# Windowed attention, forward and backward: the gradient's tile loads issued from the GpSimd queue in place of the SyncE queue

## The chip, the cores and the metric

The kernel runs on one core of one Trainium2 chip. A core has a matrix engine (PE, with its weight loads PEld), a vector engine (DVE), a scalar engine (ACT), GpSimd (POOL) and SyncE (SP), each with an instruction queue of its own that it works through in program order. DMAs are started by an instruction in one of these queues. The metric is the device time of one execution in microseconds (us); lower is better. Times are medians of several executions; the profile is of one execution.

## The reference

The input `x` is an image of 256 x 256 positions with C = 384 channels in bf16. It is cut into 8 x 8 windows of 64 positions, and each window does single-head attention; the kernel returns the output and, for a given `grad_out` of the same shape as `x`, the gradients with respect to `x`, `wqkv` and `wo`.

```python
xw  = windows(x)                       # (1024 windows, 64, 384)
qkv = xw @ wqkv                        # wqkv: (384, 1152)
q, k, v = split(qkv, 3)
p   = softmax(q @ k.T * C ** -0.5)     # 64 x 64 in each window
o   = unwindow((p @ v) @ wo)           # wo: (384, 384)
return o, *vjp(x, wqkv, wo)(grad_out)
```

## The kernel before

**Weights.** The products of weights that the windows need are formed once at the start: A = Wq Wk^T (scaled), B = Wv Wo, and their transposes AT and BT. With them the scores of a window are x A x^T, the output is P (x B), and the backward pass needs grad_out BT and x AT.

**Tiles and quads.** A tile is two windows one above the other: 16 image rows by 8 columns, 128 positions on the 128 partitions, 384 channels along the free dimension. Four tiles side by side make a quad. There are 16 bands of 32 tiles, so 512 tiles and 128 quads; `quads` (L328) lists them and `sts` holds the state of each.

**One quad's work.** `load` (L112 to L118) fetches a quad's four tiles of `x` into `xq` (L117) and its four tiles of `grad_out` into `dq` (L118), 96 KB a DMA. `load_turn` (L120 to L128) issues two DMA transposes (L127), `dT` from `dq` and `xT` from `xq`, both with the channels on the partitions. `project` (L140) multiplies `dT` by BT (kind 0) and `xT` by A (kind 1) into `yz`; ACT copies the results from PSUM (L150 for kind 0, L152 for kind 1). `to_tokens` (L154) issues a third, double-sized DMA transpose, `tok` from `yz` (L156). `scores` (L159, matmuls on L165) takes `yz` and `xT`; `soft` is the softmax and its backward on DVE and ACT; `uv` (L212, matmuls on L219) makes x B and x AT; `turn` transposes small squares on PE; `attend` (L235) makes the output and the gradient of `x` for two of the four tiles. It copies each from PSUM with ACT into the buffers `osb` (L259) and `dsb` (L263), of which the pool `ob` keeps three each, and stores each in two halves of 48 KB from POOL (L266). `gf_group` (L271) adds up the weights' gradients for groups of three quads and is fed in between by `filler`.

**The order.** The whole main loop stands under a manual schedule (L332): every engine works in exactly the order in which the code is written. Iteration i of the loop (L339 to L350) issues `load` for quad i+3, `load_turn` for quad i+2, and then one `step` in which three quads are at different stages: the quad i+1 is projected (A), the quad i goes through scores, softmax and the first half of `attend` (B), the quad i-1 through the second half of `attend` (C). The projection from `dT` comes in the middle of a step, after the `uv` matmuls (L313), and `to_tokens` near its end (L322). In the queue of SP an iteration is therefore eight tile loads, the transposes dT and xT, and the transpose tok. In the queue of POOL a step is the eight half-tile stores of the second half of `attend` for quad i-1, followed by the eight of the first half for quad i.

**Buffers.** `xq` has 10, `dq` 6, `xT` 3, `dT`, `yz` and `tok` 2 buffers. PSUM is a ring of eight banks (`ring`) that all matmul results pass through.

**Semaphores.** A DMA's landing is told by one of eight semaphores for the DMAs of SP (DMAHW0 to 7) and one of eight for those of POOL (DMASW0 to 7), taken in turn. A DMA waits, beside its data, for the landing of the DMA of its own queue that had the same semaphore, eight DMAs earlier.

Of the kernel before, what the change touches and what calls it, by code (L numbers as in the profile page):

```python
# [22 lines left out]
def kernel(  # L23
# [21 lines left out]
    nc = tc.nc  # L45
# [60 lines left out]
    def dram_tile(ap, bp, t):  # L106
        return ap[0, 2 * WIN * bp:2 * WIN * (bp + 1), WIN * t:WIN * (t + 1), :]
# [4 lines left out]
    def load(st):  # L112
        bp, t0 = st["at"]
        st["xq"] = xq = grp.tile([P, QUAD, C], BF16, tag="xq", name="xq", bufs=2 * GQ + 4)
        st["dq"] = dq = qp.tile([P, QUAD, C], BF16, tag="dq", name="dq", bufs=6)
        for t in range(QUAD):
            nc.sync.dma_start(out=xq[:, t, :], in_=dram_tile(x, bp, t0 + t))  # L117
            nc.sync.dma_start(out=dq[:, t, :], in_=dram_tile(grad_out, bp, t0 + t))  # L118

    def load_turn(st):  # L120
        xq, dq = st["xq"], st["dq"]
# [210 lines left out]
    with tc.manual_schedule(engines=MANUAL):  # L332
        for i in range(min(AHEAD, n)):
            load(sts[i])
            if i < AHEAD - 1:
                load_turn(sts[i])
        held = []
        get = lambda i: sts[i] if 0 <= i < n else None
        for i in range(-1, n + 1):  # L339
            if AHEAD <= i + AHEAD < n:  # L340
                load(sts[i + AHEAD])
            if AHEAD - 1 <= i + AHEAD - 1 < n:
                load_turn(sts[i + AHEAD - 1])
            step(get(i - 1), get(i), get(i + 1))
            if i > 0:
                held.append(sts[i - 1])
                sts[i - 1] = None
            if held and (len(held) == GQ or i == n):
                fill.append(gf_group(held))
                held = []  # L350
        filler(1 << 30)
# [60 lines left out]
```

## Time and profile before

| what | before |
|---|---|
| device time, median of 3 | 2145.26 us (2143.43 to 2146.45) |
| span of the profiled execution | 2144.9 us |
| busy PE / DVE / ACT / POOL | 95% / 64% / 68% / 53% |
| mean granted PE clock | 0.995 |
| DMA, mean over the span | 191 GB/s, 409.04 MB in 1046330 packets |

The profiled execution's span lies 0.4 us below the median of the timed runs and within their range; nothing else lies around it, so terms taken from the span can be set against the median. SP is not in the first table of the page, because everything that it does is issuing and counts as no busy time; its instructions are seen in the timeline and in the views of single lines. In those views the three numbers after a count are the shortest, the median and the longest duration in ns. In the timeline a row is: start in us, duration in us, engine, line, operation, names, count, and in brackets the idle time of the engine ahead of it with what ended it.

### The profile page before, as it was taken

Reading aid. Unit: us, or ns where it says so; the run is one execution under the profiler, and the core shown is the slowest. Engines: PE = TensorE matmul, PEld = TensorE weight load, DVE = VectorE, ACT = ScalarE, POOL = GpSimd, SP = SyncE. Lnnn points to the kernel's source line nnn. Section 1 sums busy time; section 2 is a strip of 40 time slices with the busy share of each in tenths; the row PEclk is TensorE's granted clock in tenths of the full one; section 3 lists DMA queues with packets and bytes.
Section 4 is the critical chain, followed back from the end, with each engine's and each line's share of the span. In section 5 each row is a group of like instructions: output and inputs, shape, how many; then the busy total and the mean of one; then the engine's idle time right before and its main releaser. Section 6 shows DMA issues by size and latency. Waiting matters only on the chain.

```text
span 2144.9 us, 50954 instructions
## 1 busy us (share of the span) xinstructions
PE 2029.8 (95%) x18814; PEld 1098.6 (51%) x18814; DVE 1379.5 (64%) x3235; ACT 1448.5 (68%) x3213; POOL 1137.8 (53%) x2054
## 2 busy tenths in 40 slices
PE   7899999999999999999999999999999999999998
PEld 4455555555555555555545555554555555455544
DVE  4566666666666666666666666666666666666665
ACT  5676676767666766666766767676766667676663
POOL 1555555555555555555554555555555455555544
PEclk9999999999999999999999999999999999999999
DMA  8999999999999999999999999999999999999992
GB/s 171 198 192 197 192 196 196 192 193 199 193 193 196 200 191 195 191 196 193 198 190 190 198 191 202 193 197 188 197 198 196 190 198 194 192 198 194 190 184 76
DMA packets 1046330, 409.04 MB, mean 191 GB/s; under 512 B 880704, under 2 KB 1028928, under 8 KB 1046080
## 3 DMA queue, kind: packets, MB, share of 16 engines
q1 hardware_dynamic: 947376, 304.17, 80.9%
q0 software_dynamic: 98304, 101.32, 18.2%
q8 instruction: 147, 2.41, 0.5%
q14 instruction: 103, 0.84, 0.1%
q10 hardware_dynamic: 400, 0.29, 0.0%
HBM read 101.84 MB, written 101.84 MB: 95 GB/s over the span
## 4 chain that ended last, share of the span: by engine, by line
PE 41%; DMA 26%; SPq 15%; ACT 9%; issue 5%; POOL 1%; DVE 1%; ACTq 0%; POOLq 0%
DMA dT<-dq 20%; PE pj L147 16%; PE pj L219 10%; PE pg L278 9%; SPq L117 7%; SPq L118 7%; DMA out_dram<-osb 5%; ACT yz L150 4%; ACT osb L259 3%; PE sd L165 3%; POOL out_dram L266 1%; SPq L156 1%; DMA out_dram<-dsb 1%; ACT yz L152 1%; PE pd L244 1%
## 5 line engine op out<-in xcount | busy, mean ns | idle before, releaser
L266 POOL DMA_DIRECT2D out_dram<-osb x1024 | 571.9, 563 | 933.6 <-ACT osb L259 906.3
L266 POOL DMA_DIRECT2D out_dram<-dsb x1024 | 571.9, 563 | 51.2 <-issue 20.5
L259 ACT CAST osb<-po 128x384 bf16<-128x384 f32 x512 | 249.8, 488 | 408.4 <-DMA out_dram<-osb 180.6
L280 DVE TENSOR_TENSOR GF_acc<-pg,GF_acc 128x384 f32<-128x384 f32 x258 | 143.9, 558 | 542.7 <-PE pg L278 542.7
L278 PEld LDWEIGHTS <-xq 128*128 128x128 bf16 x3072 | 300.0, 98 | 226.8 <-issue 1.6
L219 PEld LDWEIGHTS <-xT 128*128 128x128 bf16 x3072 | 291.9, 98 | 185.5 <-issue 3.6
L219 PE MATMUL pj<-B_sb,xT 128*128 128x384 bf16 x1536 | 334.6, 327 | 1.8 <-ACT dsb L263 1.8
L219 PE MATMUL pj<-AT_sb,xT 128*128 128x384 bf16 x1536 | 334.0, 327 | 0.0
L147 PE MATMUL pj<-dT,BT_sb 128*128 128x512 bf16 x1152 | 276.6, 387 | 60.4 <-DMA dT<-dq 54.2
L260 DVE CAST Uq<-pu 128x384 bf16<-128x384 f32 x512 | 283.0, 553 | 75.3 <-PE pu L251 75.3
L267 DVE CAST Wq<-pw 128x384 bf16<-128x384 f32 x512 | 280.5, 548 | 0.0
L221 ACT CAST uq<-pj 128x384 bf16<-128x384 f32 x512 | 247.5, 483 | 41.9 <-PE pj L219 37.5
L278 PE MATMUL pg<-Uq,xq 128*128 128x384 bf16 x1536 | 270.5, 326 | 0.1
L278 PE MATMUL pg<-Wq,xq 128*128 128x384 bf16 x1536 | 270.1, 326 | 0.1
L147 PE MATMUL pj<-xT,A_sb 128*128 128x512 bf16 x1152 | 269.2, 379 | 0.6
L263 ACT CAST dsb<-pd 128x384 bf16<-128x384 f32 x512 | 254.7, 497 | 7.6 <-DMA out_dram<-dsb 6.4
L221 ACT CAST vq<-pj 128x384 bf16<-128x384 f32 x512 | 250.2, 489 | 2.8 <-PE pj L219 0.5
L152 ACT CAST yz<-pj 128x512 bf16<-128x512 f32 x384 | 224.2, 585 | 32.0 <-PE pj L147 0.9
L150 ACT CAST yz<-pj 128x512 bf16<-128x512 f32 x384 | 208.4, 638 | 14.4 <-PE pj L147 13.3
L147 PEld LDWEIGHTS <-BT_sb 128*128 128x128 bf16 x1152 | 106.8, 99 | 207.2 <-DMA dT<-dq 92.2
L198 ACT COPY ps<-Pb 64x256 bf16<-64x256 bf16 x256 | 103.2, 403 | 149.6 <-DVE Pb L195 148.1
L251 PE MATMUL pu<-xq,ST 64*64 64x384 bf16 x1024 | 175.5, 336 | 0.0
(64 smaller groups left out, 2217.4 us busy)
## 6 DMA issues: line engine op xcount, KB each, us to landing
xq<-in_x_dram SPq DMA_DIRECT2D x512, 96.0 KB, 3.2
dq<-in_grad_out_dram SPq DMA_DIRECT2D x512, 96.0 KB, 3.3
out_dram<-osb POOLq DMA_DIRECT2D x1024, 48.0 KB, 3.8
out_dram<-dsb POOLq DMA_DIRECT2D x1024, 48.0 KB, 4.4
dT<-dq SPq DMA_TRANSPOSE x128, 6.5
xT<-xq SPq DMA_TRANSPOSE x128, 7.1
tok<-yz SPq DMA_TRANSPOSE x128, 7.9
w_sb<-in_wqkv_dram SPq DMA_DIRECT2D x1, 864.0 KB, 5.5
```

Source lines behind the costliest of these rows:

```text
L147: nc.tensor.matmul(pj[:].rearrange("p t w k -> p (t w k)"), lhsT=wgt[:, m, mo * P:(mo + 1) * P], rhs=src[:, :, m, :], start=(m == 0), stop ...
L150: ENG[EV["z"][mo]](out=yz[:, mo, :, 0:4:3, :], in_=pj[:])
L152: ENG[EV["y"][mo]](out=yz[:, mo, :, 1:3, :], in_=pj[:])
L219: nc.tensor.matmul(pj[:], lhsT=st["xT"][:, t, m, :], rhs=wgt[:, m, :], start=(m == 0), stop=(m == CK - 1))
L221: cp(out=dst[:, t, :], in_=pj[:])
L251: nc.tensor.matmul(dst[o, :], lhsT=st[lhs][h, t, :], rhs=st[rhs][h, t, :], start=first, stop=True)
L259: ENG[EV["o"][t]](out=osb[:], in_=po[:])
L260: ENG[EV["U"][t]](out=st["Uq"][:, t, :], in_=pu[:])
L263: ENG[EV["d"][t]](out=dsb[:], in_=pd[:])
L266: nc.gpsimd.dma_start(out=dram_tile(dst, bp, t0 + t)[WIN * w:WIN * (w + 1)], in_=src[h, :])
L267: ENG[EV["W"][t]](out=st["Wq"][:, t, :], in_=pw[:])
L278: nc.tensor.matmul(pw[:], lhsT=st["xq"][:, t, ma * P:(ma + 1) * P], rhs=st["UW"[f] + "q"][:, t, :], start=(i == 0), stop=(i == n - 1))
```

## The change

The four DMAs that fetch a quad's tiles of `grad_out` are issued from the queue of POOL (`nc.gpsimd`) in place of the queue of SP (`nc.sync`). The call stays where it is in the code, at the start of an iteration.

```diff
         for t in range(QUAD):
             nc.sync.dma_start(out=xq[:, t, :], in_=dram_tile(x, bp, t0 + t))
-            nc.sync.dma_start(out=dq[:, t, :], in_=dram_tile(grad_out, bp, t0 + t))
+            nc.gpsimd.dma_start(out=dq[:, t, :], in_=dram_tile(grad_out, bp, t0 + t))
```

In the queue of SP, one iteration in the middle of the program before, with what each instruction waits for (DMAHW and DMASW are the semaphores of SP's and POOL's DMAs):

```order
L156 DMA_TRANSPOSE tok<-yz 128x24x128 [waits DMAHW6_49,Activation_49]
L117 DMA xq<-in_x_dram 128x1x384 [waits DMAHW7_49,PE_49]
L118 DMA dq<-in_grad_out_dram 128x1x384 [waits DMAHW0_49]
L117 DMA xq<-in_x_dram 128x1x384 [waits DMAHW1_49]
L118 DMA dq<-in_grad_out_dram 128x1x384 [waits DMAHW2_49]
L117 DMA xq<-in_x_dram 128x1x384 [waits DMAHW3_49]
L118 DMA dq<-in_grad_out_dram 128x1x384 [waits DMAHW4_49]
L117 DMA xq<-in_x_dram 128x1x384 [waits DMAHW5_49]
L118 DMA dq<-in_grad_out_dram 128x1x384 [waits DMAHW6_49]
L127 DMA_TRANSPOSE dT<-dq 128x12x128 [waits DMAHW7_49]
```

The same stretch of SP's queue with the change:

```order
L156 DMA_TRANSPOSE tok<-yz 128x24x128 [waits DMAHW7_49,Activation_49]
L117 DMA xq<-in_x_dram 128x1x384 [waits DMAHW0_49]
L117 DMA xq<-in_x_dram 128x1x384 [waits DMAHW1_49]
L117 DMA xq<-in_x_dram 128x1x384 [waits DMAHW2_49]
L117 DMA xq<-in_x_dram 128x1x384 [waits DMAHW3_49]
L127 DMA_TRANSPOSE dT<-dq 128x12x128 [waits DMASW7_49,DMASW6_49,DMAHW4_49,DMASW5_49,DMASW4_49]
L127 DMA_TRANSPOSE xT<-xq 128x12x128 [waits DMAHW5_49]
```

Between tok and dT there are four loads where there were eight, and dT now waits for landings of POOL's DMAs.

In the queue of POOL, at the border between two steps, before (the last four stores of one step, the first four of the next):

```order
L266 DMA out_dram<-osb 8x8x384 [waits DMASW0_49,Activation_49]
L266 DMA out_dram<-osb 8x8x384 [waits DMASW1_49]
L266 DMA out_dram<-dsb 8x8x384 [waits DMASW2_49,Activation_49]
L266 DMA out_dram<-dsb 8x8x384 [waits DMASW3_49]
L266 DMA out_dram<-osb 8x8x384 [waits DMASW4_49,Activation_49]
L266 DMA out_dram<-osb 8x8x384 [waits DMASW5_49]
L266 DMA out_dram<-dsb 8x8x384 [waits DMASW6_49,Activation_49]
L266 DMA out_dram<-dsb 8x8x384 [waits DMASW7_49]
```

And with the change:

```order
L266 DMA out_dram<-osb 8x8x384 [waits DMASW4_49,Activation_49]
L266 DMA out_dram<-osb 8x8x384 [waits DMASW5_49]
L266 DMA out_dram<-dsb 8x8x384 [waits DMASW6_49,Activation_49]
L266 DMA out_dram<-dsb 8x8x384 [waits DMASW7_49]
L118 DMA dq<-in_grad_out_dram 128x1x384 [waits DMAHW3_49,DMASW0_49,PE_49]
L118 DMA dq<-in_grad_out_dram 128x1x384 [waits DMASW1_49]
L118 DMA dq<-in_grad_out_dram 128x1x384 [waits DMASW2_49]
L118 DMA dq<-in_grad_out_dram 128x1x384 [waits DMASW3_49]
L266 DMA out_dram<-osb 8x8x384 [waits DMASW4_49,Activation_49]
L266 DMA out_dram<-osb 8x8x384 [waits DMASW5_49]
L266 DMA out_dram<-dsb 8x8x384 [waits DMASW6_49,Activation_49]
L266 DMA out_dram<-dsb 8x8x384 [waits DMASW7_49]
```

The four loads of a later quad stand between the last store of one step and the first store of the next, in a queue that is worked through in order. At the program's start sixteen of them, for the first four quads, stand ahead of POOL's first store. Nothing changes in the order on PE, DVE and ACT.

## The prediction

> **What bounds the kernel now.** I read the page first, by engine and by chain.
>
> ```profile
> PE 2029.8 (95%) x18814; PEld 1098.6 (51%) x18814; DVE 1379.5 (64%) x3235; ACT 1448.5 (68%) x3213; POOL 1137.8 (53%) x2054
> PE 41%; DMA 26%; SPq 15%; ACT 9%; issue 5%; POOL 1%; DVE 1%; ACTq 0%; POOLq 0%
> ```
>
> PE is busy for 95% of the span, so at most 2144.9 - 2029.8 = 115 us can be won without less work on PE. But the chain that ended last stands in DMAs and in SP's queue for 41% of the span. The chain of waits in order of time shows a step where PE waits for nothing, from one quad's scores to the next, and after it one where it waits:
>
> ```profile
> 998.50 0.59 ACT yz L152
> ...
> 1018.20 6.65 DMA dT<-dq
> ...
> 1024.90 2.12 PE pj L147 x9
> ...
> 1068.20 0.86 PE sd L165 x24
> ...
> 1083.99 0.86 PE sd L165 x24
> ```
>
> The step without a wait takes 1083.99 - 1068.20 = **15.79 us**. The projection at 1024.90 starts just when the transpose dT, issued at 1018.20, lands 6.65 us later. The first and last scores say what a step takes on the average, and the same view for tok says it for SP:
>
> ```profile
> L165 PE MATMUL sd<-xT,yz x3072: 188/193/243, 20.6 to 2102.3; 128*128 128x64 bf16 x192
> L156 SPq DMA_TRANSPOSE tok<-yz x128: 3603/5592/7426, 30.2 to 2099.0; - x128
> L127 SPq DMA_TRANSPOSE dT<-dq x128: 1439/2204/3315, 9.7 to 2076.3; - x128
> L127 SPq DMA_TRANSPOSE xT<-xq x128: 1715/2778/4687, 11.4 to 2077.8; - x128
> L118 SPq DMA_DIRECT2D dq<-in_grad_out_dram x512: 552/598/1852, 2.0 to 2065.0; - x171
> ```
>
> The last scores matmul starts about 0.7 us into its step, so a step is (2101.6 - 20.6)/127 = 16.39 us, 0.60 us above 15.79. SP goes from tok to tok in (2099.0 - 30.2)/127 = 16.29 us. It is never idle in between:
>
> ```profile
> 1006.75 6.27 SPq L156 DMA_TRANSPOSE tok<-yz  x1
> 1013.06 0.59 SPq L117 DMA_DIRECT2D xq<-in_x_dram  x1
> ...
> 1018.20 2.17 SPq L127 DMA_TRANSPOSE dT<-dq  x1
> 1020.42 1.99 SPq L127 DMA_TRANSPOSE xT<-xq  x1
> 1022.51 5.35 SPq L156 DMA_TRANSPOSE tok<-yz  x1
> ```
>
> Eight loads lie between 1013.06 and dT at 1018.20, 0.64 us each; from the end of an instruction to the next 0.04 to 0.1 us pass. By the program dT is issued a whole step ahead of its use; here it is issued 6.7 us ahead, because **SP's queue has fallen behind**. PE needs 15.79 us a step, SP 16.29, and PE, gaining on SP, waits now and then.
>
> One row of the waits speaks against this reading:
>
> ```profile
> SPq L156 <- ACT yz L150: 578.1, 115, 6.3
> ```
>
> It says that tok, 5 us a step, waits for ACT. But tok waits for the last copy of its quad, on L152, and that copy ended at 998.50 + 0.59 = 999.09, 7.7 us before tok began at 1006.75; the copy named, on L150, belongs to the next quad. The 6.27 us are SP's own issuing. Were it a real wait, tok's end would be fixed by ACT, and dT would still come four loads sooner behind it.
>
> **The change part by part.** *Removed from SP:* four loads a step, each 0.60 us and 0.04 us to the next, 4 x 0.64 = 2.56 us. SP then needs 16.29 - 2.56 = 13.7 us a step against PE's 15.79, with 2.1 us to spare. It will really wait for yz, tok will go out as soon as its quad is projected, and dT some 9 us ahead of its use. What stops, then, is what PE waits for on DMAs that SP issues late:
>
> ```profile
> PE pj L147 <- DMA dT<-dq: 54.2, 58, 3.4
> PE pd L244 <- DMA tok<-yz: 4.7, 1, 4.7
> PE pj L147 <- ACT uq L221: 4.5, 3, 1.5
> PE pj L147 <- ACT ps L198: 1.0, 1, 1.0
> PE pj L219 <- ACT dsb L263: 1.8, 2, 1.1
> 1008.14 1.63 PEld L147 LDWEIGHTS <-BT_sb 128*128 128x128 bf16 x9 [1.36 <-DMA dT<-dq]
> ```
>
> The two rows of L147 that name ACT are on the same projections; at 1008.14, one of these four times, the weight load of the same matmul waited for dT (1.36 us), so I count them with it. Sum: 54.2 + 4.7 + 4.5 + 1.0 = **64.4 us**. As a check, 127 steps at 0.60 us above 15.79 are 76 us; some 12 us of that are other things (the granted clock is 0.995 in the mean, which on 2145 us makes 11 us), and I leave them in. Late next are ACT's copies, for which PE waits 1.8 us in all now (L219 for dsb).
>
> *Added to POOL:* four loads of 96 KB a step, which stand between two steps' stores.
>
> ```profile
> L266 POOL DMA_DIRECT2D out_dram<-osb x1024: 562/562/711, 38.3 to 2121.6; - x171
> POOL out_dram L266 <- ACT osb L259: 906.3, 242, 37.0
> 1052.13 1.11 POOL L266 DMA_DIRECT2D out_dram<-osb  x2 [1.35 <-ACT osb L259]
> ...
> 1062.66 1.11 POOL L266 DMA_DIRECT2D out_dram<-osb  x2 [6.09 <-ACT osb L259]
> dq<-in_grad_out_dram SPq DMA_DIRECT2D x512, 96.0 KB, 3.3
> out_dram<-dsb POOLq DMA_DIRECT2D x1024, 48.0 KB, 4.4
> ```
>
> A store of 64 rows takes POOL 0.562 us; a load there has no row. From below it costs as much as a store, 0.56 us, if the price is one for each instruction; by the rows that it moves, 128 for 64, it costs 1.12. The nearest row is the store on the same engine and it counts rows of the same 768 bytes, so I take **1.12**, the dearer of the two. Nothing excludes more: the dearest load on SP's queue took 1.852. Four loads are 4.5 us (2.2 to 7.4). The room for them: POOL's waits for osb are 906.3 us, of which 37.0 are the start and some 115 are the short one of 1.35 us between a step's two bursts; the other (906.3 - 37.0 - 155)/127 = 5.6 us a step lie just where the loads are put. They fit, and POOL is busy for 16 x 0.562 + 4.5 = 13.5 of 15.79 us.
>
> *The new waits.* A load waits for the landing of the store eight places ahead, and the store four places behind it for the load's landing. The stores of dsb land 4.4 us after their issue in the median, loads on SP's queue 3.3; eight stores take 4.5 us to issue, so this is mostly over when it is reached. dT now waits for loads on POOL; they are issued a step ahead of it. Queued behind it on SP are xT and tok, with the 2.1 us of room. DMA traffic stays the same in bytes, so I cost it at nothing; the rivals say what that is worth.
>
> The row of L266 also says that no store of osb took POOL longer than 711 ns, while DVE was busy for 64% of the span. The Trainium skill ("SBUF — State Buffer", "Who interferes with whom", and "A bandwidth-pool intuition that's wrong") has a rule against the change: GpSimd writes its DMAs' descriptors through a port that some operations of DVE lock, and a DMA of 620 ns then takes about 3100. By that figure, as an estimate, four loads would be 12.4 us, POOL 21.4 us a step, and the time 2145 + 127 x 5.0 = 2780; by the row of L266 the rule adds nothing here, and it goes with the rival in which POOL becomes the bound.
>
> *The sum:* 2144.9 - 64.4 = 2080.5 us of span, and with the 0.4 us to the median **2081**.
>
> **The rivals.**
>
> *The DMA engines are the bound (no change).* Then SP's transposes are slow because the data moves slowly, and a freed queue only makes them longer.
>
> ```profile
> q1 hardware_dynamic: 947376, 304.17, 80.9%
> q0 software_dynamic: 98304, 101.32, 18.2%
> 1038.40:1044.70 6.30, 6.30 (x39) 3.34 (x36) 4.42 (x12) 5.06 (x13) 2.53 (x5) 1.00 1.25 192
> 1044.70:1049.90 5.20, 5.07 (x56) 2.72 (x56) 2.90 (x7) 3.65 (x8) 3.55 (x7) 1.00 0.75 194
> ```
>
> For it: the two queues' packets fill 99% of the engines' time, and dT's issue stretches from 1.44 to 3.3 us. Against it: packets of two queues overlap (the share, next to last in a row of the stretches, is 1.25 while SP issues tok), and while SP issues eight loads it falls to 0.75. To bind again the three transposes, 2.2 + 2.8 + 5.6 = 10.6 us, would have to stretch by more than 2.1 us, a fifth; if they took all 2.56 us, the time would be 2145. Chance 0.08.
>
> The DMA page of the Trainium skill ("DMA: Bandwidth & Descriptors", "Issuing engines are not separate DMA queues") says the same: all queues run on the same 16 engines, and issuing from several saves only the issue time, usually small. Here the trace agrees with the first half, but this issue time is 2.56 us of the 16.29 that SP takes.
>
> *POOL becomes the bound (slower).* The place is the first store of a step behind the four loads: osb and dsb have three buffers, so ACT's copy of one tile waits for the store of the tile three before, PE's next `uv` for ACT. It decides once 16 x 0.562 + 4 loads exceed 15.79, from 1.70 us a load, and is slower than before when they exceed 16.39, from 1.85. At 2.0 us a load a step takes 17.0, and the time is 2145 + 127 x 0.6 = 2221. For it: 1.852 was seen once on SP. Against: 562 to 711 ns for every store of osb. Chance 0.07.
>
> *Stores late in some steps.* A load between 1.12 and 1.7 us, or landings slower by a third under the transposes, delays ACT by some 0.2 us a step: 127 x 0.2 = 25 us back, 2106; between 2096 and 2140. The two waits of L219 for dsb are this case already. Chance 0.17.
>
> **How the numbers follow.** The forecast, 2081, has 0.68 and a range of its own of 2068 (all steps at 15.79: 2145 - 76, nearly) to 2096. To it I add most of the late stores: low 2068, high 2124; outside lie the end of that case, the unchanged time and the slower one. About 0.2%, 4 us, is what a measurement can tell from no change. Faster: 0.68 + 0.17 = 0.85; same 0.08; slower 0.07.
>
> **What would show it.** Right: PE's wait for dT nearly gone; SP's tok to tok equal to a step, with a true gap ahead of tok; nearly all steps at 15.8 us; POOL's idle time ahead of the step's first store down from 5.6 to about 1 us. Wrong: the three transposes longer by 2 us a step (DMA engines); loads on POOL above 1.7 us, or ACT's copies on L259 and L263 waiting for stores while PE waits at L219 (POOL). A dT that waits for its loads' landing would mean that POOL runs later than I think.

## The result and the profile after

The changed kernel takes **2082.16 us** (median of 4, 2079.46 to 2084.99) against 2144.35 us before (median of 4 with the runs beside it). The ratio is 0.9722, with a 95% interval of 0.970 to 0.9744: 2.8% faster. The forecast was 2081. The profiled execution spans 2079.2 us where the one before spanned 2144.9, which is 65.7 us less.

The page of the changed kernel, busy time by engine and the chain that ended last by engine:

```profile
PE 2015.4 (97%) x18814; PEld 1103.6 (53%) x18814; DVE 1380.3 (66%) x3235; ACT 1438.7 (69%) x3213; POOL 1418.2 (68%) x2566
PE 70%; ACT 14%; DMA 9%; issue 5%; POOL 1%; DVE 0%; ACTq 0%; POOLq 0%
```

SP's queue, 15% of the chain before, is no longer in it, DMAs have gone from 26% to 9%, and PE now makes up 70%. The timeline of SP over two steps (start, duration, queue and line, operation, names, count):

```profile
1009.99 2.61 SPq L127 DMA_TRANSPOSE xT<-xq  x1
1015.46 5.23 SPq L156 DMA_TRANSPOSE tok<-yz  x1
1020.74 2.52 SPq L117 DMA_DIRECT2D xq<-in_x_dram  x4
1023.43 1.89 SPq L127 DMA_TRANSPOSE dT<-dq  x1
1025.37 2.68 SPq L127 DMA_TRANSPOSE xT<-xq  x1
1031.25 4.88 SPq L156 DMA_TRANSPOSE tok<-yz  x1
```

And that of ACT, the last copies that tok has to wait for:

```profile
1013.56 1.88 ACT L152 CAST yz<-pj 128x512 bf16<-128x512 f32 x3
1029.34 1.88 ACT L152 CAST yz<-pj 128x512 bf16<-128x512 f32 x3
```

Before, tok began 0.1 us behind xT and 7.7 us behind its data. Now xT's issue ends at 1012.60 and tok begins at 1015.46, 0.02 us after ACT's last copy ended at 1015.44, and so again at 1031.25 (copies ended at 1031.22). SP has caught up and waits for its data, 2.9 and 3.2 us in these two steps.

The views of single lines (count, then shortest, median and longest in ns, then first and last start in us):

```profile
L165 PE MATMUL sd<-xT,yz x3072: 189/193/242, 20.0 to 2036.5; 128*128 128x64 bf16 x192
L156 SPq DMA_TRANSPOSE tok<-yz x128: 3612/4432/6425, 24.4 to 2033.2; - x128
L127 SPq DMA_TRANSPOSE dT<-dq x128: 1426/1900/2985, 8.9 to 2006.8; - x128
L118 POOL DMA_DIRECT2D dq<-in_grad_out_dram x512: 518/551/680, 1.3 to 1996.2; - x171
```

Taken as before the change, with the 0.7 us of the last step left out, a step is (2035.8 - 20.0)/127 = 15.87 us, 0.08 above the 15.79 of a step without waits, where it was 0.60 above. By the starts of the scores, 111 of the 127 steps now take between 15.7 and 15.9 us; before, 48 did. A load on POOL took 0.551 us. And tok's issue, with SP's pause ahead of it, is shorter: 4.43 us in the median for 5.59.

The waits of PE (who waited for whom: us in total, times, longest):

```profile
PE pj L219 <- ACT dsb L263: 9.7, 6, 2.3
...
PE pj L219 <- ACT osb L259: 3.0, 4, 1.4
PE pd L244 <- DMA tok<-yz: 2.6, 1, 2.6
...
PE pj L147 <- DMA dT<-dq: 0.7, 1, 0.7
```

The 64.4 us of waits for dT and tok are 3.3; in their place the waits of L219 for ACT's copies have gone from 1.8 to 12.7. POOL's timeline around the loads, and its largest wait:

```profile
1007.54 2.15 POOL L118 DMA_DIRECT2D dq<-in_grad_out_dram  x4
1012.57 1.16 POOL L266 DMA_DIRECT2D out_dram<-osb  x2 [2.89 <-ACT osb L259]
```

```profile
POOL out_dram L266 <- ACT osb L259: 373.1, 207, 20.3
```

The four loads take 2.15 us of the gap between two steps' stores, and POOL still stands idle behind them; its waits for osb fell from 906.3 to 373.1 us.

### The profile page after: what moved, and what is told of

Read it like the earlier page. It is cut to its first block, busy times and chain, and to the rows that moved or that the text cites. A ratio compares the mean times of both kernels' runs of the same rounds, so it can differ in the third digit from the quotient of the medians.

```text
span 2079.2 us, 51457 instructions
## 1 busy us (share of the span) xinstructions
PE 2015.4 (97%) x18814; PEld 1103.6 (53%) x18814; DVE 1380.3 (66%) x3235; ACT 1438.7 (69%) x3213; POOL 1418.2 (68%) x2566
## 4 chain that ended last, share of the span: by engine, by line
PE 70%; ACT 14%; DMA 9%; issue 5%; POOL 1%; DVE 0%; ACTq 0%; POOLq 0%
PE pj L219 22%; PE pj L147 21%; PE pg L278 15%; ACT yz L150 8%; DMA out_dram<-osb 5%; ACT osb L259 5%; PE sd L165 5%; DMA out_dram<-dsb 2%; PE pd L244 2%; PE pu L251 2%; PE pt L230 1%; POOL out_dram L266 1%; PE pt L232 1%; DMA tok<-yz 0%; PE pc L96 0%
## 5 line engine op out<-in xcount | busy, mean ns | idle before, releaser
L266 POOL DMA_DIRECT2D out_dram<-osb x1024 | 577.9, 569 | 447.4 <-ACT osb L259 373.1
L219 PEld LDWEIGHTS <-xT 128*128 128x128 bf16 x3072 | 292.2, 98 | 198.4 <-issue 17.7
L219 PE MATMUL pj<-B_sb,xT 128*128 128x384 bf16 x1536 | 333.9, 326 | 9.9 <-ACT dsb L263 9.7
L219 PE MATMUL pj<-AT_sb,xT 128*128 128x384 bf16 x1536 | 333.8, 326 | 3.1 <-ACT osb L259 3.0
L118 POOL DMA_DIRECT2D dq<-in_grad_out_dram x512 | 273.9, 550 | 55.7 <-PE pj L147 21.9
L147 PE MATMUL pj<-dT,BT_sb 128*128 128x512 bf16 x1152 | 269.5, 379 | 0.7 <-DMA dT<-dq 0.7
L152 ACT CAST yz<-pj 128x512 bf16<-128x512 f32 x384 | 224.7, 585 | 31.9
```

The lines of the kernel that those rows point to most:

```text
L118: nc.gpsimd.dma_start(out=dq[:, t, :], in_=dram_tile(grad_out, bp, t0 + t))
L147: nc.tensor.matmul(pj[:].rearrange("p t w k -> p (t w k)"), lhsT=wgt[:, m, mo * P:(mo + 1) * P], rhs=src[:, :, m, :], start=(m == 0), stop ...
L152: ENG[EV["y"][mo]](out=yz[:, mo, :, 1:3, :], in_=pj[:])
L219: nc.tensor.matmul(pj[:], lhsT=st["xT"][:, t, m, :], rhs=wgt[:, m, :], start=(m == 0), stop=(m == CK - 1))
L266: nc.gpsimd.dma_start(out=dram_tile(dst, bp, t0 + t)[WIN * w:WIN * (w + 1)], in_=src[h, :])
```

## The experiments

The theory: SP's issue time was the bound, and the gain has a bend: once SP needs less than PE's 15.79 us a step, taking more from it brings nothing more. The rivals: the gain comes from bytes that a second DMA queue carries; it matters that the loads were those of dq; stores were the hidden limit. Each run stands beside runs of the kernel before on the same chip, whose median is given with it.

### Half and a quarter of the change

```diff
-            nc.gpsimd.dma_start(out=dq[:, t, :], in_=dram_tile(grad_out, bp, t0 + t))
+            (nc.gpsimd if t < 2 else nc.sync).dma_start(out=dq[:, t, :], in_=dram_tile(grad_out, bp, t0 + t))
```

> Two of the four dq loads of a quad on POOL, two on SP. If SP's issue time is the bound, it needs 16.29 - 2 x 0.64 = 15.0 us a step, below PE's 15.79, and the whole gain is there already: 2080 to 2092 us. If the gain came from bytes that a second DMA queue carries, half the bytes bring half the gain: about 2113 us. If POOL's loads hold up stores, this one has fewer waits of PE for dsb and osb than the full change (12.7 us there).

With `t < 1`:

> One of the four dq loads on POOL, three on SP. SP's issue time as the bound: 16.29 - 0.64 = 15.65 us a step, just below 15.79, so most of the gain: 2085 to 2105 us. Gain in proportion to the bytes on the second queue: about 2129 us.

Two loads on POOL: 2090.15 us against 2139.14 (ratio 0.9769, 0.9753 to 0.9785). One load: 2091.95 us (0.978, 0.9761 to 0.9798). Both lie in the ranges that the bend gives, and far from proportion (about 2113 and 2129): a quarter of the moved loads brings 47 us of gain, half brings 49, all four 62.

So the gain is not flat beyond the bend: all four loads are better than two by some 10 us (ratio 0.9722, 0.970 to 0.9744). With two, SP already waits for its data:

```profile
1002.10 1.89 SPq L127 DMA_TRANSPOSE xT<-xq  x1
1006.89 4.09 SPq L156 DMA_TRANSPOSE tok<-yz  x1
```

tok begins 2.9 us behind xT, 0.02 us after ACT's last copy ended at 1006.87. Most of the rest is at the start of the program: by the starts of the scores, the first five steps took 82.7 us with two loads on POOL and 75.8 with four, which is 6.9 us of the 9.8 us by which the two profiles' 127 steps differ. Behind them the two are nearly alike, as the bend has it; why the start differs stays open. PE's waits at L219, expected to be fewer here if the loads on POOL hold up stores, were 11.2 us for 12.7: not clearly fewer.

With one load on POOL, SP is still just busy all the time, as the view of tok and PE's wait show:

```profile
L156 SPq DMA_TRANSPOSE tok<-yz x128: 3855/5880/7954, 29.9 to 2048.1; - x128
```

```profile
PE pj L147 <- DMA dT<-dq: 13.3, 20, 2.5
```

From tok to tok (2048.1 - 29.9)/127 = 15.89 us, tok's issue is as long as before (5.88 us), and PE waits 13.3 us for dT where it waited 54.2.

### More issues on SP, next to no bytes

```diff
+        for e in range(2):
+            nc.sync.dma_start(out=tiny[:, e, :], in_=wo[0:16, 16 * e:16 * e + 16])
         for t in range(QUAD):
             nc.sync.dma_start(out=xq[:, t, :], in_=dram_tile(x, bp, t0 + t))
```

> The kernel before with two extra loads a quad on SP, 512 bytes each (16 rows of 32 bytes from wo into a tile that nothing reads). They add issue time on SP and next to no bytes. SP's issue time as the bound: 16.29 + 2 x 0.64 = 17.57 us a step, 127 x 1.28 = 163 us more, about 2307 us (2270 with a shorter issue of 0.5 us). If the DMA engines or the bytes are the bound: 2145 us.

2255.75 us against 2139.14 (1.0541, 1.0515 to 1.0566). Two loads of 512 bytes a quad cost 116.6 us, 0.92 us a step. The view of the extra loads:

```profile
L118 SPq DMA_DIRECT2D tiny<-in_wo_dram x256: 327/458/1495, 1.2 to 2170.5; - x128
```

Two issues at the median of 0.458 us are 0.92 us, so the price is about their issue time. That the two figures are equal is partly chance: SP goes from tok to tok in (2208.6 - 34.0)/127 = 17.12 us, 0.83 above the kernel before, since tok's own issue was 0.30 us shorter than there; and the mean granted clock fell from 0.995 to 0.984, which costs PE time. I had put 0.5 to 0.64 us on each issue, so the time came out below the figures. That issues cost time here with next to no bytes is shown by this run.

With six of them on the changed kernel:

> The changed kernel with six of the same extra 512-byte loads a quad on SP. SP was then busy for 12.6 us a step with 3.2 us of true waiting ahead of tok. SP's issue time as the bound: 12.6 + 6 x 0.64 = 16.5 us a step, above 15.79 again, so PE waits for dT again and the time goes back up to about 2160 us (2120 to 2200). If the gain came from the second DMA queue: 2082 us, since the dq loads stay on POOL.

2324.68 us (1.0846, 1.0806 to 1.0886), 165 us above the figure: the direction is right and the size is not. Its views of tok and of SP's waits say what I had left out:

```profile
L159 SPq DMA_TRANSPOSE tok<-yz x128: 3920/5712/8497, 31.1 to 2278.0; - x128
```

```profile
SPq L120 <- DMA tok<-yz: 101.1, 82, 3.8
```

(The lines are three higher here: L159 is tok, L120 the loads of x.) SP goes from tok to tok in (2278.0 - 31.1)/127 = 17.69 us where I had 16.5. First, tok's issue is back at 5.71 us, 1.28 above that of the changed kernel; it follows xT directly again. Second, 101.1 us are waits of a load of x for the landing of tok: with six more DMAs behind tok the load is the one eight places on, which has the same semaphore.

With three:

> The changed kernel with three extra 512-byte loads a quad on SP (six brought 2325 us). Each costs SP about 0.52 us by the run with six; 12.6 + 3 x 0.52 = 14.2 us a step is below PE's 15.79, and the 3.2 us that SP waits ahead of tok cover them. A bound with a bend at PE's step: no change against 2082 us, within 6. A cost that each issue on SP has, whatever the room: half of what six cost, about 2200 us.

2095.08 us against 2139.80 (0.9788, 0.9745 to 0.9831): 13 us above the changed kernel (14 us by the ratios, whose intervals just do not overlap), outside the 6 that I allowed, but nowhere near 2200. Three cost 13 us, six cost 243. This is the bend. Where the 13 us come from, the same view says:

```profile
L159 SPq DMA_TRANSPOSE tok<-yz x128: 3836/5949/7456, 28.5 to 2047.2; - x128
```

SP's pause of about 3 us is used up not by three issues of 0.42 us alone but by tok too, whose issue grows from 4.43 to 5.95 us once nothing stands between xT and it; from tok to tok it is (2047.2 - 28.5)/127 = 15.90 us, just above PE's 15.79. SP no longer pauses ahead of tok. Besides, dT is now the eighth DMA behind tok, and SP waits for tok's landing ahead of it, 16.5 us in all by the view of SP's waits.

### The other four loads

```diff
-            nc.sync.dma_start(out=xq[:, t, :], in_=dram_tile(x, bp, t0 + t))
-            nc.gpsimd.dma_start(out=dq[:, t, :], in_=dram_tile(grad_out, bp, t0 + t))
+            nc.gpsimd.dma_start(out=xq[:, t, :], in_=dram_tile(x, bp, t0 + t))
+            nc.sync.dma_start(out=dq[:, t, :], in_=dram_tile(grad_out, bp, t0 + t))
```

> The kernel before with the four x loads of a quad on POOL in place of the four dq loads, which stay on SP. SP loses the same four issues. SP's issue time as the bound: as the change, 2082 us within 8. If it mattered that the loads of dq, on which dT waits, were the ones moved (landing sooner or beside other DMAs), it stays near 2145 us.

2084.04 us against 2144.37 (0.9715, 0.9698 to 0.9733), the same as the change. Which loads leave SP does not matter.

### A fourth buffer for the stores

```diff
-    ob = ctx.enter_context(tc.tile_pool(name="ob", bufs=3))
+    ob = ctx.enter_context(tc.tile_pool(name="ob", bufs=4))
```

> The kernel before with four buffers each for osb and dsb. With SP's issue time as the bound it changes nothing: 2145 us, within 4. If the stores had been the hidden limit of the kernel before (ACT was idle 180.6 us ahead of osb with a store named as what ended it), it gains: 2120 us or less.

> The changed kernel with four buffers each for osb and dsb in place of three, so that ACT's copy of a tile waits for the store of the same tile of the quad before, a whole step earlier, and no longer for the store of the tile two places ahead in the same step. If late stores behind the loads are what is left of PE's waits (12.7 us at L219), they go: about 2070 us. If they are no more than a place where another wait ends: 2082 us.

On the kernel before: 2141.84 us against 2144.37, ratio 0.9989 (0.9967 to 1.0011), no difference. So the 180.6 us for which ACT stood idle ahead of osb there were no limit. On the changed kernel: **2065.14 us**, ratio 0.963 (0.9616 to 0.9645) to the kernel before, 17 us better than the change alone and the fastest version here. The 12.7 us of L219 are most of it; PE's busy time is also 5.0 us less (2010.4 us). Its waits of PE no longer have a row for L219, and the scores matmuls run

```profile
L165 PE MATMUL sd<-xT,yz x3072: 189/193/242, 21.7 to 2021.5; 128*128 128x64 bf16 x192
```

which is (2021.5 - 21.7)/127 = 15.75 us a step: the first steps, with fewer quads in work, are shorter, and nearly all others are at the 15.79 of PE's own work. The same edit is worth nothing while SP is the bound and 17 us once it is not.

### All eight loads on POOL

The diff is that of the change, made for L117 too.

> All eight loads of a quad on POOL, none on SP. SP has 9.8 us of issuing a step, far below 15.79, so it brings nothing more. POOL issues for 16 x 0.562 + 8 x 0.551 = 13.4 us a step, and the eight loads (4.4 us, more with the waits for landings eight DMAs back) fill the 5.6 us between two steps' stores. If stores behind the loads reach PE through the buffers of osb and dsb, PE's waits at L219 grow from 12.7 us to 50 us or more: 2115 to 2200 us. If POOL's queue is free enough: 2082 us.

2269.98 us against 2144.37 (1.0575, 1.0537 to 1.0613): slower, and by more than I had put. PE's waits are where I had put them:

```profile
PE pj L219 <- ACT dsb L263: 79.1, 46, 3.8
PE pj L219 <- ACT osb L259: 66.4, 24, 5.6
```

The mean granted clock is 0.973, which on 2272.7 us is up to 61 us more than at full clock; this I had not counted. Whether the buffers of osb and dsb are what hands the delay on was tried with a fourth one:

> All eight loads on POOL (2270 us) with four buffers each for osb and dsb in place of three. If the loads on POOL cost time because stores behind them come late to ACT through those buffers (145.5 us of PE's waits at L219), these waits go and with them the periods of half clock: 2065 to 2090 us. If POOL's queue itself is what binds (its issuing and its waits for landings eight DMAs back), it stays above 2200 us.

2364.91 us against 2139.80 (1.1026, 1.0972 to 1.1081): slower still, so the buffers are not the limit in this version. POOL's and PE's waits of this run:

```profile
POOL out_dram L266 <- DMA dq<-in_grad_out_dram: 180.7, 94, 5.2
POOL out_dram L266 <- DMA xq<-in_x_dram: 87.3, 56, 3.5
```

```profile
PE pg L278 <- ACT dsb L263: 134.4, 81, 3.9
```

POOL's stores wait 268 us for the landing of loads. Each DMA of POOL waits for the landing of the one eight places ahead; with eight loads in a row ahead of a step's first eight stores, each of these stores waits for a load. In the trace most of the late ones start 0.28 or 0.55 us after that landing. So it seems to be POOL's queue itself that binds in this version, though it issues for only 13.4 us a step. With three buffers the same two rows are 24.8 us (12.6 and 12.2), and POOL's stores wait longer for earlier stores (185.3 us); there the buffers and the queue are not told apart. That the limit is the eight DMAs in flight is read from these rows and was not tried by itself. Why four buffers are 95 us slower than three here stays open.

## Why the prediction was right, point by point

**SP was the bound: right.** The row that spoke against it, tok's 578.1 us of waiting for ACT, was a wrong attribution, as argued: the changed kernel, in which tok does wait for ACT, starts it 0.02 us after the copies on L152, and two nearly empty loads on the kernel before cost about their issue time, which a queue that had 5 us a step to spare would have hidden. The step that the theory names is seen in the traces directly: from dT's issue to the first projection that uses it there were 6.7 us in the median before, and there are 15.3 after (I had put some 9).

**The term of 64.4 us: right.** It came out as 64.4 - 3.3 = 61.1 us.

**What was left in: wrong in size.** I left some 12 us of other losses in the sum. Of PE's busy time, which the sum did not touch, 2029.8 - 2015.4 = 14.4 us went as well. The mean granted clock rose from 0.995 to 0.999, which is at most 8 to 9 us of it; the rest is not assigned.

**ACT's copies as next in line: right, but costed at nothing.** Their waits grew by 12.7 - 1.8 = 10.9 us. So the sum is -61.1 - 14.4 + 10.9 = -64.6 against the 65.7 measured; that the forecast is 1 us off is partly because two mis-sized terms cancel.

**SP's room of 2.1 us: right in sign, too simple.** I took the transposes' issue as fixed. Removing the loads also made tok 1.2 us shorter; the room became about 3 us. In the six runs in which SP pauses ahead of tok its issue took 4.2 to 4.6 us in the median, in the six in which it follows xT at once 5.3 to 5.9. The rival of the DMA engines has this much in it: part of tok's issue time seems to have been waiting behind the transposes ahead of it. It does not hold as a bound, since the transposes did not stretch to take the freed time.

**A load on POOL at 1.12 us: wrong.** It takes 0.551, the lower end; a load of 128 rows is no dearer than a store of 64. It changed nothing in the time, since both fit the gap of 5.6 us (for which the prediction takes 155 us off, 115 of the short waits at 1.35 us each). Of that gap some 3 us are left in place of the 1 us that I expected. The loads land after 5.2 us in the median (I had taken 3.3 from SP's queue), and dT, a step behind, did not notice.

**Stores late in some steps, the rival with 0.17: in part.** PE's waits at L219 are this mechanism, at 0.1 us a step and not 0.2. What makes the stores late is mostly not the loads ahead of them but a pause of POOL, below. The two waits of the kernel before, which I had counted to this rival, also come 5 to 7 us behind such a pause.

**POOL as the bound, the rival with 0.07: no**, for four loads; with eight the runs point to it, but not at 1.70 us a load as I had put it: the loads kept their 0.551 us, and the waits for landings seem to be what bound.

## What to carry to other kernels

A queue that only issues is an engine like any other: compare its time a step with that of the busiest engine, take from it until it is below, and look for the next limit there, since more brings little and a fix that was worthless before (a fourth store buffer) may now pay. Before moving DMAs to another queue, count not only the issue time there but how many of its DMAs may be in flight and how long they take to land. Check a wait that the profile names against the instruction that the program really waits for.

## What the runs showed of the hardware

**POOL pauses for 2.0 to 2.7 us every 106 DMAs.** In the timeline of POOL, after and before, instructions with an idle time that nothing in the profile ended:

```profile
618.07 0.59 POOL L266 DMA_DIRECT2D out_dram<-osb  x1 [2.47 <-issue]
702.46 0.56 POOL L266 DMA_DIRECT2D out_dram<-dsb  x1 [2.03 <-issue]
786.25 0.56 POOL L266 DMA_DIRECT2D out_dram<-osb  x1 [2.18 <-issue]
```

```profile
1022.62 0.56 POOL L266 DMA_DIRECT2D out_dram<-osb  x1 [2.47 <-issue]
1134.28 0.56 POOL L266 DMA_DIRECT2D out_dram<-dsb  x1 [2.32 <-issue]
1237.73 0.56 POOL L266 DMA_DIRECT2D out_dram<-osb  x1 [2.18 <-issue]
```

Counted in the trace, there are 106 DMAs of POOL from one such pause to the next, or a multiple of 106, in both kernels and in the other ten profiled runs, with 16 to 24 DMAs a step (the runs with three and six extra loads have one more such idle time each); hence some 84 us between them after (20 a step) and some 108 before (16 a step). A pause that falls on the first stores of a step can reach PE: behind that of 618.07 ACT's copy of dsb, and then PE, came late. Five of the changed kernel's six waits of L219 for dsb, 9.3 of the 9.7 us, come 5.9 to 11.8 us behind such a pause.

```profile
625.12 0.48 ACT L263 CAST dsb<-pd 128x384 bf16<-128x384 f32 x1 [3.02 <-DMA out_dram<-dsb]
```

```profile
625.65 0.65 PE L219 MATMUL pj<-B_sb,xT 128*128 128x384 bf16 x3 [2.29 <-ACT dsb L263]
```

What POOL does in it, the profile does not tell.

**A wait of PE can cost its clock as well.** In the kernel before, the timeline of PE and the stretch behind one of its longest waits (the column after the engines is the granted clock):

```profile
1107.15 3.81 PE L147 MATMUL pj<-dT,BT_sb 128*128 128x512 bf16 x9 [2.52 <-DMA dT<-dq]
```

```profile
1107.30:1110.70 3.40, 3.40 (x9) 1.21 (x8) 0.15 (x1) 1.17 (x2) 0.00 (x0) 0.50 1.21 235
```

After 2.52 us of idleness PE ran at half clock for 3.4 us, and nine matmuls that take 2.12 us took 3.81: the wait and the half clock together cost 4.2 us, not 2.5. After the wait of 2.29 us at 625.65 in the changed kernel the clock stayed full:

```profile
625.70:628.70 3.00, 3.00 (x18) 1.63 (x18) 1.02 (x3) 1.85 (x5) 3.00 (x6) 1.00 0.96 175
```

The Trainium skill ("TensorE: Matmul & The Clock Gate", "Part 1: The HAM clock gate") says that the clock falls to half after an idle window of about 3.4 us that runs freely. The clock of one half and the 3.4 us agree; the idle time that sufficed here is shorter than the window, 2.52 us, and in the 3.4 us ahead of the half clock PE was still busy for 0.88 us. The length of the wait does not decide by itself: in the kernel before, PE also waited 2.54 us for dT ahead of 1695.44, the clock stayed at 1.00, and the nine matmuls took 2.12 us.
